# Low parts of half the probabilities: a GpSimd subtraction replaced by ScalarE's negated copy and accumulating transfers, in units 4 to 107

## The chip, the core and the metric

The kernel runs on one core of one Trainium2 chip. Its engines are TensorE (PE in the profile; PEld is its weight load), VectorE (DVE), ScalarE (ACT), GpSimd (POOL) and SyncE (SP), which only issues transfers here. Each engine works through its own instructions in program order and waits on semaphores for the others. The metric is the device time of one execution in microseconds, the median of several runs.

## What is computed

A transformer block with conditioning: a layer norm whose scale and shift come from `c`, attention over a cached window, a gated residual, a second layer norm, and a gated ReLU network. Everything is float32. The reference, cut to what matters:

```python
mod = (silu(c) @ w_mod).reshape(1, 6, 1, -1)       # sa, ca, ga, sb, cb, gb
h = layernorm(x) * (1 + ca) + sa
q = h @ wq                                         # 2048 x 576 -> 32 heads of 128
k, v = the last 512 rows of the caches, 16 heads, each used by two heads of q
p = softmax(q @ k.T * 128 ** -0.5)                 # 2048 x 512 for each head
x = x + ga * ((p @ v) @ wo)
h = layernorm(x) * (1 + cb) + sb
gate, up = h @ W_gate, h @ W_up                    # 576 -> 4608
x = x + gb * ((gate * (gate > 0) * up) @ W_down)
```

## The kernel before

**Split operands.** To keep float32 accuracy at the matmul's faster format (`fp32r`), every operand `a` is split into a high part `hi = round(a)` and a low part `lo = a - hi`, and a product is the sum of three matmuls: hi by hi, hi by the other's lo, lo by the other's hi. The split of an operand is a cast on ACT (`hi`) and a subtraction on POOL (`lo`).

**Units.** Attention runs as 128 units. A unit is one head and one block of 512 query rows. In unit `u`, with keys on partitions (the scores stand transposed, 128 keys by 512 queries, four such tiles in two halves `h` of 2 x 512 columns):

- `s_half(u, 0)` and `s_half(u, 1)`: 12 matmuls make the scores in PSUM (lines 496 to 498), and DVE takes block maxima (line 501);
- `max_pre`, `cross`, `max_bc`: DVE forms the maximum over the keys and spreads it to all partitions (`by_moves(u)`, true for units 4 to 107, uses DVE's moves for it; the other units use PE);
- `exp_half(u, h)`: DVE subtracts the maximum (line 591), ACT takes the exponential (line 593): the probabilities `p`, 128 x 1024 for each half;
- `hi_half(u, h)`: ACT casts `p` to `hi` (line 577);
- `ksum_op(u, h)`: sums for the denominator, one addition on DVE (line 606), two on POOL (line 609);
- `lo_half(u, h)`: POOL subtracts, `lo = p - hi` (line 600), once for each half, both at the end of the unit;
- `pv_half(u, h)`: 6 matmuls each, in the unit after (lines 633 to 635). Line 635 reads `lo`.

**What sets the order.** The order on PE, DVE, ACT and POOL is written out by hand: the loop over `u` calls these functions at ten numbered places, and `run(u, k)` puts the scheduled extra steps (weight loads and splits, layer norms) between them. On PE the order within unit `u` is: scores of `u`; the query projection of `u + 1` (`qproj`, line 424, 14 matmuls); a piece of the output projection (`piece`, line 660, 12 matmuls); `pv_half(u - 1, 0)`; `pv_half(u - 1, 1)`; another piece; then the scores of `u + 1`. So the two `lo` tiles of a unit are made at its end on POOL, and PE reads them more than half a unit later. On POOL the order within a unit is: the two `ks` additions, in some units a weight split (line 183), `lo` of half 0, `lo` of half 1, in some units another weight split, `olo` (line 649, the low part of the attention output), then the `ks` additions of the next unit.

**Buffers.** `p` and `hi` have 3 buffers, `lo` has 2, one for each half, so that `lo` of half 1 in unit `u` overwrites that of unit `u - 1`.

**Transfers.** All transfers are issued from SP and ACT. During the units they bring weights and keep split weights in DRAM for later use. POOL issues none. After the units follows the gated network (lines 1016 and later), which the change leaves as it is.

Of the kernel before, what the change touches and what calls it, by code (L numbers as in the profile page):

```python
# [7 lines left out]
F32 = mybir.dt.float32  # L8
F32R = mybir.dt.float32r
I32 = mybir.dt.int32  # L10
AF = mybir.ActivationFunctionType
ALU = mybir.AluOpType
AX = mybir.AxisListType

P = 128
# [19 lines left out]
def kernel(  # L35
# [13 lines left out]
    nc = tc.nc  # L49
# [433 lines left out]
    st_, t5, pt, hi_, lo_, bc, rb, ks_, pvps, done, o, bps = ({} for _ in range(12))  # L483
# [21 lines left out]
    def by_moves(u):  # L505
        return PE0 <= u < MOVES
# [90 lines left out]

    def lo_half(u, h):
        lo_[u, h] = pp.tile([P, 2, 512], F32R, tag="lo", name=f"lo{u}_{h}", bufs=2)
        nc.gpsimd.tensor_sub(lo_[u, h], pt[u, h], hi_[u, h].bitcast(F32))  # L600

    def ksum_op(u, h):
        p = pt[u, h]
# [852 lines left out]
    for i, ab in enumerate(lay0 + lay):  # L1456
        n = i - len(lay0) - 2 * NFT + 4
# [193 lines left out]
    for u in range(NU):  # L1651
# [61 lines left out]
        hi_half(u, 1)  # L1713
        flush(pend_act)
        lo_half(u, 0)
        lo_half(u, 1)
        run(u, 9)
    for u in range(NU, NU + 8):
# [55 lines left out]
```

## Time and profile before

| | |
|---|---|
| three runs | 2855.35, 2856.07 and 2860.0 us, median 2856.07 us |
| profiled execution, first to last instruction | 2855.8 us |
| granted TensorE clock | 0.998 |
| PE, DVE, ACT, POOL busy | 99%, 79%, 52%, 74% of the span |
| units 4 to 107 | from 92 to 1344 us of the span, the last unit's `pv` until about 1356 us |
| an undisturbed unit | 11.83 us from scores to scores |

The profile page gives the busy time of each engine, the span in 40 slices, the transfer queues, the chain of work that ended last, and the costliest groups of instructions. A group's row reads: line, engine, operation, output tile <- input tiles, sizes, count | busy us, mean ns of one | idle time of the engine just before, and who ended it. A row of the timeline reads: start in us, length in us, engine, line, operation, tiles, count, and in brackets the idle time before it. Consecutive equal instructions are merged into one row. `SPq` and `ACTq` are transfers being issued.

### The profile page before, as it was taken

How to read it: one execution, taken by the hardware profiler on the slowest of the kernel's cores; microseconds unless marked ns; L12 is line 12 of the kernel's file. 1: busy time of each engine (PE TensorE's matmuls, PEld its weight loads, DVE VectorE, ACT ScalarE, POOL GpSimd, SP SyncE). 2: the span in 40 equal slices, each digit the busy share in tenths (PEclk: the TensorE clock that was granted, in tenths of full speed). 3: DMA queues.
4: the chain of work that ended last, by engine and by line, in shares of the span. 5: the costliest groups of instructions: out<-in, count | busy, mean ns of one | idle time of the engine just before them, and what ended most of it. 6: DMA issues, size and time to landing. Idle time of an engine off the chain costs nothing.

```text
span 2855.8 us, 41174 instructions
## 1 busy us (share of the span) xinstructions
PE 2815.0 (99%) x15006; PEld 2449.5 (86%) x15006; DVE 2246.8 (79%) x3384; ACT 1476.7 (52%) x2105; POOL 2123.8 (74%) x1564
## 2 busy tenths in 40 slices
PE   6999999999999999999999999999999999999999
PEld 5788888888888888888888888888888888888888
DVE  7899999999889998888889756676677466666666
ACT  5766666666766666666656444444444122222221
POOL 5688888888899989877778766788777356656653
PEclk9999999999999999999999999999999999999999
DMA  4012132222232213312243456666667844444442
GB/s 163 24 45 79 65 106 85 83 82 100 95 104 94 92 62 131 105 70 80 68 155 139 150 213 229 231 240 231 234 234 261 338 165 154 155 155 159 159 154 106
DMA packets 164506, 399.57 MB, mean 140 GB/s; under 512 B 15056, under 2 KB 62160, under 8 KB 164304
## 3 DMA queue, kind: packets, MB, share of 16 engines
q1 hardware_dynamic: 132912, 284.69, 29.9%
q10 hardware_dynamic: 31392, 112.26, 10.0%
q8 instruction: 118, 1.93, 0.3%
q14 instruction: 84, 0.69, 0.1%
HBM read 271.16 MB, written 154.57 MB: 149 GB/s over the span
## 4 chain that ended last, share of the span: by engine, by line
PE 83%; DVE 6%; POOL 5%; issue 2%; ACT 2%; DMA 2%; SPq 0%; ACTq 0%; DVEq 0%; POOLq 0%
PE gu L1016 26%; PE wo L660 12%; PE qps L424 11%; PE md L660 8%; PE st_P L1118 6%; PE s L498 3%; PE s L497 3%; PE s L496 3%; PE pv L635 3%; PE pv L634 3%; PE pv L633 3%; POOL lo L600 2%; DVE t L501 1%; DVE p L591 1%; POOL wop L795 1%
## 5 line engine op out<-in xcount | busy, mean ns | idle before, releaser
L600 POOL TENSOR_TENSOR lo<-p,hi 128x1024 fp32r<-128x1024 f32 x256 | 610.6, 2406 | 1.1 <-ACT hi L577 1.1
L609 POOL TENSOR_TENSOR ks<-ks,p 128x512 f32<-128x512 f32 x256 | 351.7, 1374 | 238.7 <-DVE ks L606 135.5
L501 DVE TRANSPOSE_TENSOR_REDUCE t<-s 128x32 f32<-128x1024 f32 x256 | 313.8, 1239 | 85.9 <-PE s L498 76.6
L1016 PE MATMUL gu<-hop_B,wop 128*128 128x512 f32 x1512 | 375.0, 391 | 0.2 <-POOL wop L795 0.2
L1016 PEld LDWEIGHTS gu<-hop_B,wop 128*128 128x128 f32 x1512 | 274.9, 188 | 51.1 <-POOL wop L795 0.9
L1016 PE MATMUL gu<-hop_T,wop 128*128 128x512 f32 x1260 | 316.1, 391 | 0.0
L424 PE MATMUL qps<-hTa,wA 128*128 128x512 f32 x1288 | 312.9, 394 | 3.1 <-DVE hTa L372 1.6
L660 PE MATMUL wo<-woga,ohi 128*128 128x288 f32 x1472 | 298.8, 295 | 2.0 <-POOL woga L183 1.4
L591 DVE TENSOR_TENSOR p<-s,mb 128x1024 f32<-128x1024 f32 x246 | 290.3, 1219 | 4.2
L424 PEld LDWEIGHTS qps<-hTa,wA 128*128 128x128 f32 x1288 | 244.5, 190 | 56.6 <-DVE hTa L372 3.2
L476 ACT ACTIVATE qhi<-qps 128x512 fp32r<-128x512 f32 x128 | 76.4, 597 | 366.9 <-PE qps L424 358.4
L660 PEld LDWEIGHTS wo<-woga,ohi 128*128 128x128 f32 x1472 | 245.9, 188 | 18.8 <-POOL woga L183 3.4
L1016 PEld LDWEIGHTS gu<-hop_T,wop 128*128 128x128 f32 x1260 | 227.8, 188 | 39.0
L577 ACT CAST hi<-p 128x1024 fp32r<-128x1024 f32 x256 | 259.5, 1042 | 1.5
L660 PE MATMUL md<-wogb,hhi 128*128 128x288 f32 x1272 | 256.9, 295 | 0.4 <-DVE acc L671 0.4
L593 ACT ACTIVATE p<-p 128x1024 f32<-128x1024 f32 x246 | 249.5, 1051 | 13.7 <-DVE p L591 13.4
L671 DVE TENSOR_TENSOR acc<-md,acc 128x576 f32<-128x576 f32 x159 | 119.9, 755 | 160.4 <-PE md L660 159.8
L660 PEld LDWEIGHTS md<-wogb,hhi 128*128 128x128 f32 x1272 | 210.9, 188 | 12.6 <-DVE acc L671 1.4
L1127 DVE TENSOR_TENSOR acc<-st_P,acc 128x576 f32<-128x576 f32 x160 | 121.1, 757 | 127.9 <-PE st_P L1118 127.9
L660 PE MATMUL wo<-woga,olo 128*128 128x288 f32 x736 | 217.8, 296 | 1.3 <-POOL olo L649 1.2
L660 PE MATMUL md<-wogb,hlo 128*128 128x288 f32 x636 | 187.5, 295 | 0.0
L649 POOL TENSOR_TENSOR olo<-rb,ohi 128x512 fp32r<-128x512 f32 x128 | 167.4, 1308 | 15.2 <-ACT ohi L645 15.0
(283 smaller groups left out, 7095.3 us busy)
## 6 DMA issues: line engine op xcount, KB each, us to landing
wop<-wk_P SPq DMA_DIRECT2D x133, 640.0 KB
wk_P<-wop ACTq DMA_DIRECT2D x119, 640.0 KB
wr<-wlay SPq DMA_DIRECT2D x68, 384.0 KB
rogb<-wd SPq DMA_DIRECT2D x68, 288.0 KB
againq<-akq SPq DMA_DIRECT2D x18, 640.0 KB
rwA<-wq SPq DMA_DIRECT2D x32, 320.0 KB
wlay<-wg SPq DMA_DIRECT2D x36, 256.0 KB
roga<-wo SPq DMA_DIRECT2D x32, 288.0 KB
```

The costliest lines, as they stand in the source:

```text
L424: return [lambda i=i, a=a, b=b: nc.tensor.matmul(ps, a, b, start=(i == 0), stop=(i == n - 1)) for i, (a, b) in enumerate(ops)]
L501: nc.vector.tensor_reduce(t5[u][:, 2 * h:2 * h + 2, :].rearrange("p k b -> p (k b)"), t.rearrange("p k (b j) -> p (k b) j", j=32), axis=AX ...
L577: nc.scalar.copy(hi_[u, h], pt[u, h])
L591: nc.vector.tensor_tensor(p, t, bc[u][:, None, :].to_broadcast([P, 2, 512]), op=ALU.subtract)
L593: nc.scalar.activation(p, p, AF.Exp, bias=0.0, scale=1.0)
L600: nc.gpsimd.tensor_sub(lo_[u, h], pt[u, h], hi_[u, h].bitcast(F32))
L609: nc.gpsimd.tensor_tensor(ks_[u], ks_[u], p[:, j, :], op=ALU.add)
L649: nc.gpsimd.tensor_sub(olo[u], o.pop(u), ohi[u].bitcast(F32))
L660: nc.tensor.matmul(ps[:, half, :H2], a[:, sl], w[b][:, cs], start=(n == 0 and seed is None), stop=(n == 5), skip_group_check=seed is not None)
L1016: nc.tensor.matmul(ps, a, c, start=s not in heir(m) and i == 0 and s not in seeds_of(m), stop=i == len(ops) - 1, skip_group_check=True)
L1118: nc.tensor.matmul(ps[:, j, :H2], x[:, sl], w[:, y, :], start=n == 0 and not second, stop=n == 2, skip_group_check=True)
L1127: nc.vector.tensor_tensor(t, ps[:, :, :H2], t, op=ALU.add)
```

## The change

In units 4 to 107 the low part of half 1 is made in another way. ACT writes `-round(p)` into the `lo` tile (an `ACTIVATE` with scale -1 whose output type is `fp32r`). Then two transfers issued from POOL's queue, one for partitions 0 to 63 and one for 64 to 127, add `p` to it (`accum_op=ALU.add`): each moves 64 rows of 4096 bytes. The sum is the same `p - hi`. Half 0, and both halves of the other 24 units, are made as before.

```diff
 
     def lo_half(u, h):
         lo_[u, h] = pp.tile([P, 2, 512], F32R, tag="lo", name=f"lo{u}_{h}", bufs=2)
-        nc.gpsimd.tensor_sub(lo_[u, h], pt[u, h], hi_[u, h].bitcast(F32))
+        if h == 0 or not by_moves(u):
+            nc.gpsimd.tensor_sub(lo_[u, h], pt[u, h], hi_[u, h].bitcast(F32))
+            return
+        nc.scalar.activation(lo_[u, h], pt[u, h], AF.Copy, bias=0.0, scale=-1.0)
+        for r in (slice(0, 64), slice(64, P)):
+            nc.gpsimd.dma_start(lo_[u, h].bitcast(F32)[r].rearrange("p k n -> p (k n)"),
+                                pt[u, h][r].rearrange("p k n -> p (k n)"), accum_op=ALU.add)
 
     def ksum_op(u, h):
         p = pt[u, h]
```

POOL's instructions around units 5 and 6, before (a name ends in a buffer's running number; `lo_0` and `lo_1` are the two halves, `kv` and `wA` are weight splits):

```order
L649 TENSOR_TENSOR olo_1384<-rb_1256,ohi_1382 128x512
L609 TENSOR_TENSOR ks_1407<-ks_1407,p_1_1397 128x512 x2
L600 TENSOR_TENSOR lo_0_1438<-p_0_1393,hi_0_1400 128x1024
L600 TENSOR_TENSOR lo_1_1440<-p_1_1397,hi_1_1436 128x1024
L183 TENSOR_TENSOR kv_0_1442<-rkv_0_1304,kv_0_1442 128x512
L649 TENSOR_TENSOR olo_1448<-rb_1403,ohi_1446 128x512
L609 TENSOR_TENSOR ks_1530<-ks_1530,p_1_1520 128x512 x2
```

The same place on POOL with the change:

```order
L655 TENSOR_TENSOR olo_1386<-rb_1256,ohi_1384 128x512
L615 TENSOR_TENSOR ks_1409<-ks_1409,p_1_1399 128x512 x2
L601 TENSOR_TENSOR lo_0_1440<-p_0_1395,hi_0_1402 128x1024
L605 DMA lo_1_1442<-p_1_1399 64x1024 x2
L183 TENSOR_TENSOR kv_0_1446<-rkv_0_1306,kv_0_1446 128x512
L655 TENSOR_TENSOR olo_1452<-rb_1405,ohi_1450 128x512
L615 TENSOR_TENSOR ks_1534<-ks_1534,p_1_1524 128x512 x2
```

The second subtraction has become the issue of two transfers at the same place of POOL's queue, behind the subtraction of half 0. The line 635 matmuls (now 641) that read `lo_1` wait for the two transfers' semaphores instead of POOL's.

ACT's instructions at the end of unit 7 and the start of unit 8, before (`acc` and `wo` are copies around the output projection, `ohi` the high part of an attention output, `qhi` that of the queries):

```order
L577 CAST hi_1_1676<-p_1_1642 128x1024
L669 COPY acc_129<-wo_0_1637 128x576
L693 COPY wo_1_1679<-acc_129 128x2x288
L182 CAST kv_1_1687<-rkv_1_1566 128x512
L645 CAST ohi_1691<-rb_1648 128x512
L476 ACTIVATE qhi_1737<-qps_1722 128x512
```

With the change:

```order
L577 CAST hi_1_1682<-p_1_1648 128x1024
L675 COPY acc_129<-wo_0_1643 128x576
L699 COPY wo_1_1685<-acc_129 128x2x288
L603 ACTIVATE lo_1_1689<-p_1_1648 128x1024
L182 CAST kv_1_1695<-rkv_1_1572 128x512
L651 CAST ohi_1699<-rb_1654 128x512
L476 ACTIVATE qhi_1745<-qps_1730 128x512
```

One instruction more stands on ACT, behind the copies that wait for PE's second piece and ahead of `ohi` and `qhi`. PE's and DVE's instructions and their order are the same; a `p` buffer is now also held until the transfers that read it have landed.

## The prediction

> **What bounds the kernel now.** I read the busy times first, then the same for the stretch of the changed units, then what PE waited for there.
>
> ```profile
> PE 2815.0 (99%) x15006; PEld 2449.5 (86%) x15006; DVE 2246.8 (79%) x3384; ACT 1476.7 (52%) x2105; POOL 2123.8 (74%) x1564
> ```
>
> ```profile
> 92.20:1356.20 1264.00, 1256.10 (x6558) 1086.16 (x6557) 1144.55 (x1948) 850.44 (x1169) 1074.26 (x660) 1.00 0.25 85
> ```
>
> The second row is the table by stretches for units 4 to 107: length, then PE, PEld, DVE, ACT and POOL busy, granted clock, share of the transfer engines, GB/s. PE is busy 1256.1 of 1264.0 us: only 7.9 us are left idle. POOL is busy 85% and ACT 67%, so both have time over, and taking work from POOL can only help where PE waits for POOL:
>
> ```profile
> PE wo L660 <- POOL woga L183: 1.4, 3, 0.7
> PE wo L660 <- POOL olo L649: 1.2, 5, 0.5
> PE pv L635 <- POOL lo L600: 1.1, 2, 0.6
> ```
>
> These are all of PE's waits for POOL in the stretch (us in total, times, longest): 3.7 us. With all idle time gone, 7.9 us would be saved, 0.3%. This is the whole upside. The downside has no such lid: PE is the bound, and the change puts a transfer on a path that PE reads from. So the question is when `lo` of half 1 arrives, against when PE wants it.
>
> **How much room there is.** One undisturbed unit on the timeline:
>
> ```profile
> 1239.20 4.76 POOL L600 TENSOR_TENSOR lo<-p,hi 128x1024 fp32r<-128x1024 f32 x2
> 1236.60 0.39 PE L496 MATMUL s<-qhi,againk 128*128 128x512 f32 x1
> 1245.94 0.39 PE L635 MATMUL pv<-lo,againv 128*128 128x512 f32 x1
> 1248.43 0.39 PE L496 MATMUL s<-qhi,againk 128*128 128x512 f32 x1
> ```
>
> POOL's first subtraction ends at 1239.20 + 2.38 = 1241.58, the second at 1243.96. PE's third line 635 matmul of the unit, the first that reads half 1, starts at 1245.94. Today half 1 is ready 1.98 us early. With the change the transfers are issued where the second subtraction began, so their whole time, from POOL being free to PE being released, has W = 1245.94 - 1241.58 = 4.36 us. Call that time D; the subtraction's D is 2.4 us. The room is not the same in all units. The tightest kind, then the first and the last of the changed units:
>
> ```profile
> 847.14 4.74 POOL L600 TENSOR_TENSOR lo<-p,hi 128x1024 fp32r<-128x1024 f32 x2
> 851.94 0.50 PE L635 MATMUL pv<-lo,kv 128*128 128x512 f32 x1 [0.57 <-POOL lo L600]
> 109.84 4.72 POOL L600 TENSOR_TENSOR lo<-p,hi 128x1024 fp32r<-128x1024 f32 x2
> 119.61 0.39 PE L635 MATMUL pv<-lo,kv 128*128 128x512 f32 x1
> 1346.74 4.75 POOL L600 TENSOR_TENSOR lo<-p,hi 128x1024 fp32r<-128x1024 f32 x2
> 1353.72 0.39 PE L635 MATMUL pv<-lo,againv 128*128 128x512 f32 x1
> ```
>
> W is 2.4, 7.4 and 4.6 us here. I worked it out so for all 104 units: mean 3.63 us, 24 units under 3.0, 27 over 4.2, and only 4 above 5.0. In the tight units a weight split stands ahead of the subtractions on POOL.
>
> **What a late transfer costs.** Not D - W in each unit. The next scores follow this read after 2.49 us on PE (1245.94 to 1248.43), and the following unit's read comes 9.34 us after its scores (1236.60 to 1245.94). If PE waits x for unit u, the scores of u + 2 and the read of unit u + 1 move back by x, but the `lo` of u + 1 does not: its scores were done before the wait. So unit u + 1 has W + x of room. The wait of a unit is max(0, D - W - wait of the unit before), and late transfers cost about half of D - W for each unit. Summed in this way over the 104 values of W:
>
> - D = 3.0: 7 us; 4.0: 37 us; 5.2: 88 us; 6.2: 137 us; 6.9: 173 us; 7.6: 209 us; 9.0: 281 us.
>
> **The change part by part.** Removed: 104 subtractions on POOL, 2.4 us each by the first row below, 250 us of POOL time. At most the 3.7 us that PE waits for POOL hang on it, and I take nothing, since `ks` starts only when its operands come.
>
> ```profile
> L600 POOL TENSOR_TENSOR lo<-p,hi 128x1024 fp32r<-128x1024 f32 x210 | 501.4, 2408 | 1.1 <-ACT hi L577 1.1
> L609 POOL TENSOR_TENSOR ks<-ks,p 128x512 f32<-128x512 f32 x210 | 287.7, 1370 | 178.8 <-DVE ks L606 117.1 <-ACT p L593 31.5 <-ACT hi L577 22.0
> L593 ACT ACTIVATE p<-p 128x1024 f32<-128x1024 f32 x210 | 211.5, 1051 | 6.3 <-DVE p L591 6.1
> L591 DVE TENSOR_TENSOR p<-s,mb 128x1024 f32<-128x1024 f32 x210 | 247.5, 1220 | 3.7
> L476 ACT ACTIVATE qhi<-qps 128x512 fp32r<-128x512 f32 x105 | 62.7, 597 | 329.3 <-PE qps L424 320.8 <-DVE t L534 8.5
> ```
>
> POOL already stands 178.8 us idle ahead of `ks`, so a POOL that is done earlier only waits longer there, and `lo` of half 0 comes no earlier.
>
> Added on ACT: 104 negated copies at 1.05 us, the time of ACT's other 128x1024 `ACTIVATE` (third row), 109 us. They stand ahead of `qhi`, before which ACT idles 329.3 us over 105 times, 3.1 us each (last row). That idle time hides them. Behind them in ACT's queue come weight casts, `ohi` and `qhi`; `ohi` may be 1.05 us later, which its reader on POOL, now free 2.4 us earlier less the two issues, makes up. Without that cover it would be at most the 109 us. The copy itself is ready in time:
>
> ```profile
> 1238.23 0.64 ACT L693 COPY wo<-acc 128x576 f32<-128x576 f32 x1
> ```
>
> The copy would end at 1238.87 + 1.05 = 1239.92 here, 1.7 us before POOL reaches the issue.
>
> Added on POOL: 208 transfers of 262,144 bytes. The trace has none from POOL and none that adds, so D comes from transfers of the other queues.
>
> ```profile
> 0.72 0.39 SPq L100 DMA_DIRECT2D cT<-c  x1
> 1.17 1.84 SPq L108 DMA_DIRECT2D acc<-x  x4
> ...
> 2.37 0.21 ACT L112 ACTIVATE sT<-cT 128x5 f32<-128x5 f32 x1 [0.37 <-DMA cT<-c]
> 4.42 0.82 DVE L285 BATCH_NORM_STATS2 sta<-acc 128x6 f32<-128x288 f32 x2 [1.22 <-DMA acc<-x]
> ...
> q10 hardware_dynamic: 31392, 112.26, 10.0%
> ```
>
> A load of 20-byte rows takes 2.37 - 0.72 = 1.65 us from issue to its reader's start: the fixed part. A 288 KB load, first of four, takes 4.42 - 1.17 = 3.25 us. ACT's queue moved 112.26 MB in 10.0% of the 16 engines' 2855.8 us: 393 GB/s while it ran. The two halves are 524,288 bytes, 1.33 us at that rate.
>
> - Lower end: 1.65 + 1.33 = 3.0 us, if adding costs nothing and nothing else moves. I see no gain below that: it holds one crossing of the data at the queue's own rate and nothing else.
> - Value: an add has to read what stands in the destination too, 2.67 us, and the stretch's other transfers hold 25% of the engines (the 0.25 of the second row quoted): 2.67 / 0.75 = 3.56. D = 1.65 + 3.56 = 5.2 us. The second issue (0.46 us by `acc`'s four) lies beside the first half's data. Between ends as far apart as 3.0 and 9.0 it is the one built on this stretch's own row and on the rate of a whole queue, which rests on more packets than the single load at the start.
> - Upper end: the halves one after the other, 2 x (1.65 + 1.78) = 6.9 us, and with the 288 KB load's slope (1.6 us for it, so 2.85 for a half read twice) 2 x 4.5 = 9.0 us.
>
> The Trainium skill, page "DMA: Bandwidth & Descriptors", section "Anatomy of one DMA — SWDGE (gpsimd) path", gives 2.0 us plus bytes at 436 GB/s for a transfer issued from GpSimd. That would make an estimate of D = 3.2 us for data that moves once and 4.4 us for twice, and 12 or 52 us in the sum; no transfer of this trace tests it.
>
> **Sum.** 2.4 us of subtraction goes, D = 5.2 us comes in its place: 88 us of new waits on PE, ACT's copies hidden, POOL's relief nothing. 2856 + 88 = **2944 us**, slower by 3%. The sum is against the profiled execution's 2855.8 us, which is 0.3 us from the median of the runs (2856.07), so I add to 2856.
>
> **Rivals.**
>
> 1. *Halves one after the other.* If the second transfer's issue or data must wait until the first has drained, D = 6.9 us and the time is 2856 + 173 = 3029 us, up to 3137 with D = 9.0. For it: both go through one queue. Against it: SP's four `acc` loads were issued 0.46 us apart, without waiting for each other to land (3.25 us).
> 2. *Issue held up by VectorE.* DVE is busy 1144.55 of 1264 us. If POOL could not prepare a transfer while one of DVE's long operations runs (1.22 us, one subtraction of line 591, fourth row of the groups above), two issues would add up to 2.4 us: D = 7.6, 2856 + 209 = 3065 us. Against it: today's `lo` takes the same 2.4 us beside a DVE that is 91% busy, so they do not shut each other out. The Trainium skill, page "SBUF — State Buffer", section "SBUF: two separate sides", says that a GpSimd-issued DMA cannot have its descriptors written while DVE runs a two-port operation; which of these DVE operations are of that kind no row shows.
> 3. *Quick transfers.* Adding is done on the way at full rate: D = 3.0 to 4.0, 2863 to 2893 us.
> 4. *Hidden.* D below 3.0: at 2.8 the sum is 3 us, and the time stays within 2850 to 2862. For it: W is 4.36 us in the undisturbed unit. Against it: 1.65 + 1.33.
> 5. *POOL's relief shows* (the faster side). The place is the weight splits and `olo` behind the old second subtraction: they start 2.4 us earlier less the issues, and PE's waits for them go. Price: 3.7 us up to 7.9 us, 2848 to 2852. It decides only if D stays under 2.6 us, where the sum of new waits is 1 us.
>
> **How the numbers follow.** 0.2% (5.7 us) is about what a measurement of this kernel can tell from no change. Forecast, D from 4.0 to 6.2 (2893 to 2993): 0.52. Rival 1: 0.18. Rival 2: 0.05. Rival 3: 0.10, all of it slower by over 0.2%. Rival 4: 0.08, the same. Rival 5: 0.07, faster. So slower 0.85, same 0.08, faster 0.07. The range reaches from rival 3's D = 3.0, 2863, to rival 2's 3065; outside it lie rivals 4 and 5 and the top of rival 1.
>
> **What would show it.** In the profile after: PE waits at line 641 for the transfers, about 80 of 104 times and some 0.9 us each (88 / 104 on the average), often in every second unit; units of 12.6 us instead of 11.83; ACT's idle time before `qhi` down by about 1 us each; POOL's idle time before `ks` up; the chain that ended last holding transfers instead of `lo`. The step on the halved cost is wrong if the waits come in each unit at full D - W. The estimate of D is wrong if the first read of half 1 starts without a wait, or if its distance from the end of `lo` of half 0 is far from 5.2 us. The cover on ACT is wrong if `ohi` or `qhi` is waited for more than today.

## The result, and the profile after

| | before | after |
|---|---|---|
| median | 2855.71 us (2854.43 to 2860.0, 4 runs) | 3393.45 us (3391.82 to 3397.64, 4 runs) |
| ratio, 95% interval | 1 | 1.1878 [1.1862, 1.1895] |
| profiled span | 2855.8 us | 3390.0 us |

Slower, as forecast, but by 538 us and not by 88: far above the range. In what follows, "before" and "after" stand for the two kernels. The page of after, with the busy time of the engines, the granted TensorE clock in 40 slices (tenths), the queue of POOL's transfers (packets, MB, share of 16 engines' span), and the groups of the transfers and of the matmuls that read them:

```profile
PE 2976.0 (88%) x15006; PEld 2568.5 (76%) x15006; DVE 2283.8 (67%) x3384; ACT 1585.5 (47%) x2209; POOL 2041.5 (60%) x1668
...
PEclk9898888888888999998999999999999999999999
...
q0 software_dynamic: 16640, 54.54, 15.5%
...
L605 POOL DMA_DIRECT2D lo<-p x208 | 172.4, 829 | 669.9 <-issue 322.7
L641 PE MATMUL pv<-lo,kv 128*128 128x512 f32 x368 | 175.1, 476 | 318.7 <-DMA lo<-p 290.0
```

Two things stand here. PE went from 99% busy to 88%, with most of the new idle time ahead of line 641, where it reads the transferred low part. And PE's busy time itself rose from 2815.0 to 2976.0 us with the same 15006 matmuls: each took longer, and the clock row falls to 8 in slices of the changed units alone.

The table by stretches for the 104 changed units, from their first scores to the first scores behind them, first of before and then of after (columns as in the prediction):

```profile
92.12:1344.00 1251.88, 1243.97 (x6495) 1075.57 (x6493) 1134.70 (x1933) 842.92 (x1160) 1065.74 (x655) 1.00 0.25 85
```

```profile
94.82:1868.61 1773.79, 1402.09 (x6494) 1192.83 (x6493) 1172.40 (x1929) 950.94 (x1262) 985.59 (x758) 0.90 0.47 91
```

The units are 521.9 us longer. PE's idle time in them rose from 7.9 to 371.7 us (+363.8), its busy time by 158.1 us. Of the 12.3 us more by which the whole span grew, 2.7 lie ahead of these units and 9.6 behind them; they were not followed up. The list of waits of after names what PE, POOL and ACT stood for (us in total, times, longest):

```profile
ACT acc L675 <- PE wo L666: 466.3, 160, 9.8
...
PE pv L641 <- DMA lo<-p: 335.2, 91, 8.5
POOL lo L605 <- issue: 322.7, 79, 5.9
...
POOL lo L605 <- ACT lo L603: 188.7, 81, 6.2
```

POOL waits twice in a unit: for ACT's negation ahead of the first issue, and, with nothing in the profile that holds it ("issue"), ahead of the second. The chain of work that ended last shows one unit of it in order of time (start, us, what):

```profile
852.03 4.49 DMA lo<-p
...
856.65 0.47 PE pv L641
...
858.08 2.87 PE wo L666 x12
...
860.97 0.65 ACT acc L675
...
862.22 1.06 ACT lo L603
863.28 0.40 issue
863.69 0.83 POOL lo L605
864.52 3.86 issue
...
868.40 4.62 DMA lo<-p
...
873.16 0.47 PE pv L641
```

From PE's read of one unit (856.65) to that of the next (873.16) 16.5 us pass. PE's second piece, ACT's copies of it and the negation behind them come first; then the first issue at 863.69, the second 4.71 us later, and 4.76 us from there to PE's read. Over the 104 units the second issue comes 4.80 us after the first (median), and PE reads 4.71 us after the second. The landing of a single transfer takes 4.4 to 7.8 us, median 4.5, and the second issue starts 0.32 us behind the landing of the first transfer (0.26 to 0.32 in all 104 units).

The table by stretches around that wait of PE shows the other half of the loss:

```profile
852.30:856.60 4.30, 0.35 (x2) 0.00 (x0) 2.49 (x5) 3.74 (x4) 3.42 (x4) 1.00 0.61 61
856.60:860.90 4.30, 4.25 (x17) 4.03 (x18) 0.69 (x1) 0.00 (x0) 3.32 (x2) 0.60 0.00 0
860.90:865.20 4.30, 4.30 (x21) 3.54 (x20) 2.70 (x4) 3.30 (x5) 0.83 (x1) 1.00 0.10 10
```

PE stands idle for 4 us, works the next 4.3 us at a granted clock of 0.60 (0.50 from 857.40 to 860.75), and is back at 1.00 behind that. The 12 `wo` matmuls of the chain take 2.87 us in the slow stretch; in the chain of before twelve of them take 1.58 us.

### The profile page after: what moved, and what is told of

Same layout as the page of the kernel before. It is cut to its first block, busy times and chain, and to the rows that moved or that the text cites. A ratio compares the mean times of both kernels' runs of the same rounds, so it can differ in the third digit from the quotient of the medians.

```text
span 3390.0 us, 41742 instructions
## 1 busy us (share of the span) xinstructions
PE 2976.0 (88%) x15006; PEld 2568.5 (76%) x15006; DVE 2283.8 (67%) x3384; ACT 1585.5 (47%) x2209; POOL 2041.5 (60%) x1668
## 3 DMA queue, kind: packets, MB, share of 16 engines
q0 software_dynamic: 16640, 54.54, 15.5%
## 4 chain that ended last, share of the span: by engine, by line
PE 57%; DMA 14%; issue 13%; ACT 6%; POOL 6%; DVE 4%; ACTq 0%; SPq 0%; POOLq 0%; DVEq 0%
PE gu L1022 21%; DMA lo<-p 12%; PE wo L666 10%; PE md L666 6%; PE st_P L1124 5%; PE qps L424 4%; PE pv L641 3%; ACT lo L603 2%; POOL lo L605 2%; PE pv L640 1%; PE s L496 1%; PE pv L639 1%; ACT acc L675 1%; PE s L497 1%; PE s L498 1%
## 5 line engine op out<-in xcount | busy, mean ns | idle before, releaser
L605 POOL DMA_DIRECT2D lo<-p x208 | 172.4, 829 | 669.9 <-issue 322.7
L641 PE MATMUL pv<-lo,kv 128*128 128x512 f32 x368 | 175.1, 476 | 318.7 <-DMA lo<-p 290.0
L615 POOL TENSOR_TENSOR ks<-ks,p 128x512 f32<-128x512 f32 x256 | 338.0, 1320 | 183.3 <-DVE ks L612 99.3
L601 POOL TENSOR_TENSOR lo<-p,hi 128x1024 fp32r<-128x1024 f32 x152 | 366.8, 2420 | 1.1 <-ACT hi L577 1.1
L675 ACT COPY acc<-wo 128x576 f32<-128x576 f32 x233 | 149.3, 641 | 466.5 <-PE wo L666 466.3
L666 PE MATMUL wo<-woga,ohi 128*128 128x288 f32 x1472 | 362.1, 341 | 0.0
L641 PEld LDWEIGHTS pv<-lo,kv 128*128 128x128 f32 x368 | 78.7, 214 | 367.0 <-ACT hi L577 199.8
L666 PEld LDWEIGHTS wo<-woga,ohi 128*128 128x128 f32 x1472 | 307.4, 234 | 21.0
L647 DVE TENSOR_TENSOR rb<-pv,rb 128x512 f32<-128x512 f32 x128 | 88.1, 688 | 264.0 <-PE pv L641 263.7
L666 PE MATMUL wo<-woga,olo 128*128 128x288 f32 x736 | 249.3, 339 | 0.0
```

Source lines behind the costliest of these rows:

```text
L605: nc.gpsimd.dma_start(lo_[u, h].bitcast(F32)[r].rearrange("p k n -> p (k n)"), pt[u, h][r].rearrange("p k n -> p (k n)"), accum_op=ALU.add)
L615: nc.gpsimd.tensor_tensor(ks_[u], ks_[u], p[:, j, :], op=ALU.add)
L641: nc.tensor.matmul(ps, v[:, kt, :], b[:, j, :], start=False, stop=(kt == 3))
L666: nc.tensor.matmul(ps[:, half, :H2], a[:, sl], w[b][:, cs], start=(n == 0 and seed is None), stop=(n == 5), skip_group_check=seed is not None)
L675: nc.scalar.copy(av, ps[:, :, :H2])
```

## The experiments

All change the kernel after, but for e10, which changes the one before. The kernel before ran beside each on the same chip, at 2854 to 2864 us. A time without a ratio (e3 to e6, e9 and e10) is that of one execution. D is the time from the end of `lo` of half 0 to PE's read of half 1, as in the prediction; the distance is the part of it from the first issue to that read.

**e1: ACT's copy alone.** The transfers are replaced by POOL's addition.

```diff
-        for r in (slice(0, 64), slice(64, P)):
-            nc.gpsimd.dma_start(lo_[u, h].bitcast(F32)[r].rearrange("p k n -> p (k n)"),
-                                pt[u, h][r].rearrange("p k n -> p (k n)"), accum_op=ALU.add)
+        nc.gpsimd.tensor_tensor(lo_[u, h], lo_[u, h].bitcast(F32), pt[u, h], op=ALU.add)
```

> One part alone: ScalarE's negated copy stays, and GpSimd adds p to it by one tensor operation in place of the two transfers. Theory A (the whole loss is the transfers and what they delay; the copy is hidden in ScalarE's idle time): 2852 to 2870 us. Rival (the copy itself costs its 1.05 us in each of 104 units, as it stands ahead of qhi and ohi): about 2856 + 109 = 2965 us.

2861.45 us, ratio 1.001 [1.0, 1.002]. The stretch of the units:

```profile
91.82:1344.01 1252.19, 1243.95 (x6494) 1075.45 (x6493) 1134.58 (x1933) 941.37 (x1263) 1065.83 (x655) 1.00 0.26 85
```

ACT is 98 us busier and the units are as long as before, 1252.19 us, as expected. As work the copy is hidden; the loss comes from the transfers.

**e2: the negation earlier**, directly behind the split of half 1 and ahead of ACT's copies that wait for PE: `lo_neg` takes both `lo` tiles and negates half 1, and `lo_half(u, 1)` only issues the transfers.

```diff
         hi_half(u, 1)
+        lo_neg(u)
         flush(pend_act)
         lo_half(u, 0)
         lo_half(u, 1)
```

> The negated copy is issued directly behind the cast of half 1, ahead of the two copies that wait for TensorE's second piece; the rest is the changed kernel. Theory A (the copy waits for a piece that itself stands behind the late read, so that transfers, read, piece, copies and negation form one loop within a unit, 16.5 us on the chain; with it undone only the late transfers remain, at half of D - W as predicted, with the measured D of 9.6 us): 310 us of waits and some 60 to 130 us of slower TensorE clock, 3220 to 3300 us. Rival (the place of the copy does not matter, each late transfer costs its full lateness by itself): 3393 us, no change by over 1%.

3330.17 us, ratio 1.1646 [1.1623, 1.1669]: 63 us better than after, less than expected. The negation now ends 3.8 us ahead of the first issue (median), so it is late no more, and yet most of the loss stays. The timeline of POOL shows why:

```profile
880.91 2.40 POOL L608 TENSOR_TENSOR lo<-p,hi 128x1024 fp32r<-128x1024 f32 x1 [3.08 <-PE pv L647]
883.25 0.83 POOL L611 DMA_DIRECT2D lo<-p  x1
888.23 0.82 POOL L611 DMA_DIRECT2D lo<-p  x1 [4.15 <-issue]
```

The 4.98 us between the issues are still there, and the subtraction of half 0 ahead of them has now become late itself (line 608 waits for PE's read of the unit before).

**e3: four transfers of 32 rows.**

```diff
-        for r in (slice(0, 64), slice(64, P)):
+        for r in (slice(i, i + 32) for i in range(0, P, 32)):
```

> The changed kernel with four transfers of 32 rows in place of two of 64. Theory A (a transfer can be issued while the ones before are under way as long as their descriptors fit together in a small ring; two of 64 rows do not, three of 32 rows do): the first three issues stand about 0.85 us apart, the fourth waits, D falls from 9.6 to about 7 to 8 us, the time to 3130 to 3300 us. Rival (each transfer of GpSimd's queue waits until the one before has landed): four landings of over 3 us each in a row, D about 13 us, 3600 to 3800 us.

**e4: no addition.** The transfers copy `p`; adding it onto the negated high part is left out.

```diff
-                                pt[u, h][r].rearrange("p k n -> p (k n)"), accum_op=ALU.add)
+                                pt[u, h][r].rearrange("p k n -> p (k n)"))
```

> The changed kernel with the addition left out of the transfers, which only copy p over the negated high part: the low part of half 1 is not formed. Theory A (adding makes a 4096-byte row take 651 ns on its transfer engine instead of the 159 ns of a copied row, 2.0 us for each of the two transfers): rows at about 160 ns, landing 2.5 us after the issue instead of 4.5, D about 5.5 us, and the time near the 2944 us predicted for 5.2 us, 2920 to 3030 us. Rival (the time is the queue's fixed cost, whatever the rows do): landing still over 4 us and over 3300 us.

**e5: more room for descriptors**, as after else.

```diff
-            rr = sp.tile([P, 16, 2], F32R, tag="rr", name=f"rr{u}", bufs=1)
+            rr = t5[u][:, 9:11, :].rearrange("p a b -> p (a b)").rearrange("p (b s) -> p b s", s=2).bitcast(F32R)
...
-    nc = bacc.Bacc("TRN2", target_bir_lowering=False, num_devices=1, dynamic_dma_scratch_size=256)
+    nc = bacc.Bacc("TRN2", target_bir_lowering=False, num_devices=1, dynamic_dma_scratch_size=384)
```

> The kernel after, with a descriptor area for GpSimd's transfers of 384 instead of 256 bytes per partition (a small tile of the first four units goes into another one to make room); transfers, negation and their order are as after. Theory A (the second accumulating transfer waits for room that the first one's descriptors hold): the second issue comes some 0.8 to 0.9 us after the first instead of 4.75, both transfers run side by side, the distance from the first issue to PE's read of the low part falls from 9.6 us to about 7 (their rows still share the engines), a unit from 16.6 to about 14 us, the time to 3080 to 3220 us. Rival B (the second issue waits for the first transfer's landing, whatever the room): nothing changes, 3390 us. Rival C (the queue works its rows off at one rate, so that an earlier issue lands no earlier): the gap goes, the distance stays at 9 us or more, 3350 us or more.

e3 took 3250.11, e4 3012.74, e5 3189.58 us, all three within the times expected by theory A. POOL's issues in one unit of the timeline of each, e3, e4 and e5 in this order (start, us, count, idle time before):

```profile
853.60 2.39 POOL L605 DMA_DIRECT2D lo<-p  x3 [4.88 <-ACT lo L603]
857.39 0.77 POOL L605 DMA_DIRECT2D lo<-p  x1 [1.40 <-issue]
```

```profile
854.39 1.07 POOL L605 DMA_DIRECT2D lo<-p  x2 [4.51 <-ACT lo L603]
```

```profile
854.74 1.70 POOL L605 DMA_DIRECT2D lo<-p  x2 [3.92 <-ACT lo L603]
```

Three adding transfers of 32 rows are issued without a pause, and the fourth waits: it starts 0.31 us behind the landing of the first (0.25 to 0.31 in all 104 units). Two copies of 64 rows are issued without a pause, and so are two adding ones once there is half as much room again. So the second issue of after waits for room that the first transfer's descriptors hold until it has landed. In rows, with 256 bytes: 96 that add find room, 128 that add do not, 128 that copy do. The rule that the next issue waits for the last transfer, whatever the room, falls with e3 and e5. The pause was worth 204 us (3393 to 3190). With it gone the distance is 7.9 us (median) instead of 9.6, against about 7 expected; in e3 it is 8.4, against 7 to 8.

The queue's row of e4's page stands against the 15.5% of after:

```profile
q0 software_dynamic: 16640, 54.54, 7.4%
```

With all of the queue's time put on its 13,312 rows of 4096 bytes (104 x 128), a row holds its engine 0.155 x 16 x 3390.0 / 13,312 = 0.63 us when it adds and 0.27 us when it copies, in transfers of 64 rows.

The stretches of the units of e3, e4 and e5, in this order, from which the table in the next section takes PE's idle and busy time:

```profile
94.07:1736.26 1642.19, 1356.20 (x6494) 1153.87 (x6493) 1172.28 (x1930) 949.69 (x1264) 1140.68 (x965) 0.92 0.46 98
95.25:1492.79 1397.54, 1285.41 (x6494) 1098.65 (x6493) 1128.29 (x1929) 944.24 (x1262) 924.00 (x756) 0.97 0.40 115
90.36:1663.69 1573.33, 1338.56 (x6494) 1135.14 (x6493) 1134.86 (x1933) 950.49 (x1264) 993.96 (x761) 0.94 0.51 102
```

**e6 and e7: transfers first.** e2, with the two issues ahead of half 0's subtraction; e7 has e5's room too.

```diff
-        lo_half(u, 0)
-        lo_half(u, 1)
+        for h in (1, 0) if by_moves(u) else (0, 1):
+            lo_half(u, h)
```

> As e2 (negation directly behind the split of half 1), and both transfers are issued ahead of GpSimd's subtraction of half 0 instead of behind it; the descriptor area stays at 256. Theory A (a unit's length is a chain of one unit: PE's read of the low part, GpSimd's subtraction, two issues, the landing): the transfers start some 2.4 to 4 us earlier against PE's read, the distance stays at 9.5 to 10 us, some 2 to 4 us of each wait go, and the time falls from 3330 to 2960 to 3130 us. Rival (the transfers' rate is the limit, not their place in the queue): 3280 us or more.

> As e6, with the descriptor area of 384 as in e5. Theory A: the issues come 0.8 us apart, the distance is about 7 us, and with the start moved ahead of the subtraction by 2.4 us or more against a room of 4.4 us behind it, nearly nothing is waited for: 2850 to 2930 us, PE's waits for the transfer under 60 us. Rival (with the adding the rows take too long in any place, or the traffic slows the other transfers): 2980 us or more.

e6 took 3222.16 us, above what theory A expected and below the rival; the waits of PE and POOL in it:

```profile
POOL lo L611 <- issue: 464.6, 105, 6.8
...
PE pv L647 <- POOL lo L608: 208.4, 91, 5.9
...
PE pv L647 <- DMA lo<-p: 35.3, 37, 2.8
```

The transfers are nearly in time now, but the second issue keeps POOL's queue waiting for 464.6 us, and half 0's subtraction, which stands behind it in the queue, is what PE waits for: a new wait in the old one's place. e7 took 3004.02 us, ratio 1.0499 [1.0468, 1.0529], above theory A's range and in the rival's (2980 or more). The wait for half 0 is nearly gone (4.0 us), and the transfers' own is back:

```profile
PE pv L647 <- DMA lo<-p: 99.7, 64, 4.6
```

**e8, e9 and e11: what e7 still loses.** e9 is e7 without the addition (left out as in e4). e8 is e7 with the transfers and the negation for the last 512 columns only, POOL subtracting the other 512; e11 is e8 with one transfer of 128 rows.

e8 against e7:

```diff
-            nc.scalar.activation(lo_[u, 1], pt[u, 1], AF.Copy, bias=0.0, scale=-1.0)
+            nc.scalar.activation(lo_[u, 1][:, 1, :], pt[u, 1][:, 1, :], AF.Copy, bias=0.0, scale=-1.0)
...
-            nc.gpsimd.dma_start(lo_[u, h].bitcast(F32)[r].rearrange("p k n -> p (k n)"),
-                                pt[u, h][r].rearrange("p k n -> p (k n)"), accum_op=ALU.add)
+            nc.gpsimd.dma_start(lo_[u, h].bitcast(F32)[r, 1, :], pt[u, h][r, 1, :], accum_op=ALU.add)
...
+        if by_moves(u):
+            nc.gpsimd.tensor_sub(lo_[u, 1][:, 0, :], pt[u, 1][:, 0, :], hi_[u, 1][:, 0, :].bitcast(F32))
```

e11 against e8:

```diff
-        for r in (slice(0, 64), slice(64, P)):
-            nc.gpsimd.dma_start(lo_[u, h].bitcast(F32)[r, 1, :], pt[u, h][r, 1, :], accum_op=ALU.add)
+        nc.gpsimd.dma_start(lo_[u, h].bitcast(F32)[:, 1, :], pt[u, h][:, 1, :], accum_op=ALU.add)
```

> As e7, and the transfers carry the last 512 of the 1024 columns of half 1 alone, in rows of 2 KB; ScalarE negates these columns only, and GpSimd subtracts the other 512 behind half 0's. Theory A: rows of about half the time, a distance of 4.5 to 5.5 us, landing well ahead of PE's read: no waits for it, 2848 to 2866 us, no gain from the 1.1 us of relief on GpSimd in each unit, since PE hardly waited for GpSimd before. If GpSimd's relief does count: 2840 us or less. Rival (rows cost by their number, not their bytes): a distance of 7 us or more, with waits as in e7.

> As e7 (both transfers ahead of half 0's subtraction, descriptor area 384), but the transfers copy p without adding (the addition is left out). Theory A (what e7 still loses comes from the time that the adding rows take): a distance of 5 to 6.5 us instead of 8.2, PE's waits for the transfer under 25 us instead of 100, the time 2862 to 2900 us. Rival (the new order itself costs, by two issues ahead of half 0's subtraction or by the negation ahead of ScalarE's copies): 2950 us or more, with PE's waits at half 0's low part or for ScalarE.

> As e8 (512 columns by an accumulating transfer ahead of half 0's subtraction, 512 by GpSimd), with one transfer of 128 rows in place of two of 64. Theory A: one issue of about 1 us less on GpSimd in each unit and a landing about as early; half 0's subtraction comes 1 us earlier, PE's waits for it and for the transfer shrink, and the time falls from 2901 to 2855 to 2885 us; not below the kernel before, since PE hardly waits for GpSimd there. Rival (a transfer of 128 rows lands later than two of 64): 2901 us or more. If it is under 2853 us, GpSimd's relief counts after all.

e9 took 2891.69 us, within the time expected, and PE waits 24.5 us for the transfers (the distance is 6.7 us, a little above the 5 to 6.5 expected): adding costs e7 112 us, so e7's rival was right in its first half, the adding rows. e8 took 2900.97 us, ratio 1.0139 [1.0109, 1.0168], more than expected. Its transfers have both landed 5.1 us after the first issue (median), as expected, but PE waits for them in some units, and in others for half 0's subtraction, behind the two issues. Two rows of its waits, then the stretch of its units:

```profile
PE pv L646 <- DMA lo<-p: 12.4, 18, 1.9
...
PE pv L646 <- POOL lo L608: 6.8, 14, 1.0
```

```profile
95.82:1384.91 1289.09, 1257.72 (x6494) 1074.10 (x6493) 1147.01 (x1929) 896.71 (x1261) 1118.15 (x858) 1.00 0.42 104
```

PE is idle 31.4 us here, 23.5 more than before; it is also 13.7 us busier, at a clock of 1.00, which was not followed up. The rows of POOL's queue in e8 and in e11, in this order, again with all of its time put on 13,312 rows, now of 2048 bytes:

```profile
q0 software_dynamic: 16640, 27.28, 7.5%
```

```profile
q0 software_dynamic: 14976, 27.27, 5.4%
```

That is 0.26 us a row in e8, less than half of the 0.63 us of 4096 bytes, so the rival by which rows cost by their number falls. In e11 it is 0.19 us for the same rows: in one transfer of 128 rows a row is quicker than in two of 64. So part of the 0.63 us of after may come from the cut into two halves and not from adding; no run has rows of 4096 bytes in one transfer of 128 rows.

e11 took 2869.78 us, ratio 1.0036 [1.0026, 1.0047], as expected. Its page and the stretch of its units:

```profile
PE 2818.9 (98%) x15006; PEld 2452.0 (85%) x15006; DVE 2247.7 (78%) x3384; ACT 1530.4 (53%) x2209; POOL 2096.1 (73%) x1668
```

```profile
93.44:1357.58 1264.14, 1247.65 (x6494) 1077.94 (x6493) 1135.84 (x1930) 896.24 (x1262) 1038.35 (x756) 1.00 0.38 106
```

This is the best form that was found, and it is still slower by 0.4%: it relieves POOL of 28 us in all, which PE did not wait for, and adds 8.6 us of idle PE (16.5 against 7.9).

**e10: a wait without traffic.** The kernel before, with one small transfer of a corner of `lo` onto itself behind half 1's subtraction.

```diff
         nc.gpsimd.tensor_sub(lo_[u, h], pt[u, h], hi_[u, h].bitcast(F32))
+        if h and by_moves(u):
+            nc.gpsimd.dma_start(lo_[u, h].bitcast(F32)[0:16, 0, 0:256], lo_[u, h].bitcast(F32)[0:16, 0, 0:256])
```

> The kernel before (GpSimd subtracts both halves; nothing on ScalarE is added), and behind half 1's subtraction in units 4 to 107 GpSimd issues one transfer of 16 KB that copies a corner of the low parts onto itself, so that PE has to wait for its landing. It moves almost no bytes: the distance D is 2.4 us of subtraction, 0.5 of issue and some 2 of landing, 4.8 to 5.5 us by the prediction's count. The prediction's rule (a wait shortens the next one, so that D-W counts in about half the units): 70 to 103 us, 2927 to 2960 us, waits in about 80 units. Rival (each unit pays its D-W in full): 125 to 196 us, 2985 to 3055 us. If the granted clock falls after each wait whatever causes it, the clock in the stretch of these units is under 1.00 here too, though no transfer adds and the traffic is as before; if it is the traffic of the transfers that lowers it, it stays at 1.00.

3013.74 us: by its total in the rival's range, above the rule's, with waits in 59 units and not in about 80. The row of these waits, and the stretch of the units, which says what the total hides:

```profile
PE pv L637 <- DMA lo<-lo: 103.3, 59, 5.8
```

```profile
93.77:1495.10 1401.33, 1287.39 (x6494) 1098.87 (x6493) 1155.70 (x1929) 846.91 (x1160) 1123.69 (x758) 0.97 0.24 77
```

PE's idle time rose by 106 us (113.9 against 7.9), close to the rule's sum; another 43 us are PE's busy time, at a clock of 0.97, though the transfer engines move less than before (77 against 85 GB/s). So the clock follows the waits and not the traffic. e9's units say the same from the other side, with 29.8 us of idle PE, a clock of 1.00 and 126 GB/s:

```profile
93.28:1371.72 1278.44, 1248.61 (x6494) 1074.37 (x6493) 1127.28 (x1930) 940.03 (x1262) 927.07 (x756) 1.00 0.43 126
```

## Why the prediction was wrong

**PE is the bound and has no more to gain: right.** e11 relieves POOL by 28 us and gains nothing; no run relieves POOL without a transfer's waits beside it, so the gain of relief alone stays unmeasured.

**A late transfer costs half: right.** The prediction's rule was wait = max(0, D - W - wait before), since a wait gives the next unit more room. In the traces the room of a unit is that of before plus 1.1 to 1.5 us for each us that the unit before waited (after, e3, e4, e5 and e10, correlation 0.89 to 0.96; that it is over 1 fits the slower clock behind a wait, which gives room too). With the D that each kernel shows in the units that wait (median), and W, the room, as in the kernel before:

| kernel | D, us | rule, us | each unit in full, us | idle PE added, us | busy PE added, us | busy per idle |
|---|---|---|---|---|---|---|
| e10 | 5.3 | 94 | 176 | 106 | 43 | 0.41 |
| e4 | 6.1 | 131 | 253 | 104 | 41 | 0.40 |
| e5 | 8.6 | 263 | 521 | 227 | 95 | 0.42 |
| e3 | 9.6 | 313 | 621 | 278 | 112 | 0.40 |
| after | 12.0 | 438 | 871 | 364 | 158 | 0.43 |

The rule comes within 26% of the idle time in all five; the full price is 1.7 times the idle time for e10 and over twice for the others. D is taken from each kernel here, so this tests the halving and not D. "Often in every second unit" did not hold for after: with D so long PE waits at this read in all 104 units (in 91 of them the list names the transfer), 3.6 us on the average, somewhat less than half of D - W.

**D = 5.2 us: the step that failed.** It was 12.0, in three pieces:

- *"The second issue (0.46 us by `acc`'s four) lies beside the first half's data."* It came 4.8 us after the first, for want of room for descriptors. This is rival 1, held down to 0.18 by a row of SP's queue, which says nothing of POOL's. Its first D, 6.9, had the mechanism and too small a transfer; its upper D, 9.0, made of 4.5 us for each half, is near the 9.6 us from the first issue to PE's read, and lacks the third piece. Rival 2 falls: in e5 the same two issues stand 0.56 us apart (at most 0.85) beside the same DVE operations.
- *The rate.* The estimate let a row that adds take twice the data time, 2.67 / 0.75 us for both halves. One half alone takes 4.4 us at least to land, and with both under way at once (e5) PE reads 7.9 us after the first issue. The Trainium skill, page "DMA: Bandwidth & Descriptors", section "Anatomy of one DMA — SWDGE (gpsimd) path", would give 2.6 us for one half as an estimate; e4's copies come near it with 2.8 us at least (median 3.9), adding ones do not. The Trainium skill, page "Collectives: The Full Stack", section "The bandwidth ceiling: the fold count and why AG ≠ RS ≠ AR", says of the add in a collective that it takes two source reads and two read descriptors for each chunk. The runs fit that: 0.63 against 0.27 us for a row, and room for two transfers that copy but not for two that add.
- *"The copy itself is ready in time."* True in the undisturbed unit it was read from. Once PE waits, its second piece is late, ACT's copies of that piece too, and the negation stands behind them: POOL waited 188.7 us for it in 81 units, and the first issue comes 2.1 us after the end of half 0's subtraction (mean), the rest of D. e2 prices it at 63 us, the least of the three.

The three prices do not add up, since each depends on the others: the room alone gives 204 us (e5), no addition gives room and rate together, 381 us (e4).

**A term that was missing: the clock.** The sum counted waits of PE only. Behind them PE is granted half its clock for 3.4 us or a multiple of it (348 of the 1773.8 us in after), and over the five kernels of the table that adds 0.40 to 0.43 us of PE time for each us of waiting, 158 us in after. In e2, e6 and e7 it adds 0.34 to 0.48. On the forecast's 88 us of waiting it would have been some 36 us, by itself still within the range. It depends on the length of the gap: in the clock records of the units of after, e4, e5 and e10, a grant of 0.5 stands within 2 us behind none of 115 gaps of 0.6 to 2 us between the starts of two matmuls, 62 of 116 gaps of 2 to 3.5 us, and 96 of 98 longer ones. The Trainium skill, page "TensorE: Matmul & The Clock Gate", section "HAM oscillation — how this bites in real kernels", warns of idle gaps of over 3.4 us, behind which PE starts again at half rate; the trace agrees, 0.60 granted in the stretch above, and shows the halved clock behind shorter gaps too, by the counts just given.

**The sum again.** With D = 12.0 in the rule 438 us, measured 364 of idle PE; the clock 158; outside the units 12; together 534, the difference of the two spans. Of what was forecast to be seen, waits at line 641 for the transfers came true, 91 of them at 3.7 us in place of 80 at 0.9, and so did the transfers on the chain that ended last (12% of the span); units are 16.6 us (median) and not 12.6. In the stretch of the units ACT's idle time before `qhi` did not shrink (326.1 us before, 334.4 after), and POOL's before `ks` fell instead of rising (176.1 to 124.3).

## What to carry to other kernels

Before a transfer takes the place of an operation, measure issue to landing for that transfer, issued from that engine's queue, with as many in flight as the kernel will have: an issue that finds no room for its descriptors stops everything queued behind it, and a transfer that adds needs more room and time than one that copies. Where PE is the bound, price each us of new waiting at about 1.4 us, as in these five kernels, if the gaps reach 2 to 4 us, and let a wait shorten the next one before summing. An operation that is ready in time in an undisturbed unit may stand, in its queue, behind what the new wait delays.

## What the runs showed that was not expected

- A row of 4096 bytes in a transfer of 64 rows holds a transfer engine 0.63 us when it is added and 0.27 us when it is copied, both between two tiles of the on-chip memory. An added row of 2048 bytes takes 0.26 us in two transfers of 64 rows and 0.19 us in one of 128.
- With 256 bytes of descriptor room per partition, two transfers of 64 rows go out 0.5 us apart if they copy and 4.8 us apart if they add; three adding ones of 32 rows go out together, and 384 bytes take two of 64.
- An issue costs POOL 0.83 us in after, where it adds, and 0.54 us in e4, where it copies, so two adding issues take two thirds of the time of the subtraction that they replace (2.4 us). Behind another that is under way an adding issue takes longer: 1.10 us for e5's second.
- PE's granted clock halves behind many waits of 2 to 3.5 us and nearly all longer ones, though the kernel is dense otherwise, whether PE waits for transfers that add or for one of 16 KB (0.97 over e10's units).
